# Batch 0 of a linear-attention and expert kernel: the query maxima subtracted by TensorE in PSUM, not by VectorE in SBUF

## The chip, the core and the metric

One Trainium2 chip, one core. The metric is the time of one execution in microseconds (us) on the device. The engines named below: PE (TensorE, matrix products; PEld is its weight load), DVE (VectorE), ACT (ScalarE), POOL (GpSimd) and SP (which issues most DMAs). Each engine works through its own queue in order; engines wait for each other by semaphores. PSUM has eight banks of 128 x 512 floats here.

## The reference, cut to what matters

Four batches of linear ("performer") attention over 8 heads, 576 tokens and 64 dimensions; then a dense layer of 2304 tokens (512 to 2048 to 512); then a layer of eight experts that is routed by argmax. The change touches the features of q:

```
def phi(x):                                   # x: q or k, scaled
    proj = np.einsum('bhsd,md->bhsm', x, omega)
    sq = np.sum(x * x, axis=-1, keepdims=True) / 2.0
    h = proj - sq
    h = h - np.max(h, axis=-1, keepdims=True)  # maximum over the 128 features
    return np.exp(h) / np.sqrt(m)
q_p, k_p = (phi(q_s), phi(k_s))
kv = np.einsum('bhsm,bhsd->bhmd', k_p, v)
num = np.einsum('bhsm,bhmd->bhsd', q_p, kv)   # divided by den = q_p . sum(k_p)
```

The term `sq` is the same for all features of a token, so it falls out when the maximum is taken away, and the kernel doesn't compute it.

## The kernel before

**Attention.** A batch is worked in four pairs of heads (p = 0 to 3). A pair of q lies as 128 rows, 64 for each of its two heads r, by 576 tokens. For k, the projection puts tokens on the partitions (L372), DVE takes the maxima (L378), ACT the exponentials (L393), and `k_kv` (L409) makes the 128 x 65 state kv, which ACT copies out of PSUM (`kv_copy`, L415). For q the projection puts the 128 features on the partitions:

- `q_proj` (L430): per head two products of 288 columns each, in four PSUM banks; the two heads use the two halves of the array's rows.
- `q_copy` (L458): ACT copies them to an SBUF tile `pr` of 128 x 576 for each head, and the banks are free.
- `q_max` (L466): POOL's partition_all_reduce puts the maximum over the features of each token into all 128 rows of a tile `mx`.
- `q_sub` (L471): DVE computes pr - mx. `q_exp` (L475): ACT takes the exponential of all 576 columns.
- `x_num` (L485, PE) multiplies by kv, `x_div` (L496 to L499, DVE) divides, `x_turn` (L508, PE) transposes, `x_hi` (L516, ACT) and `x_lo` (L520, DVE) write the result as a high and a low part, xh and xl.

The tiles `pr` have three buffers and a pair takes two, so the projections of pair p + 1 start when `x_num` of pair p has read its tiles.

**The dense layer.** A step (c, f) is `mm1` (L615) of a chunk of tokens and 128 of the 2048 hidden units, then the gate on ACT and DVE, then `mm2` (L646). Chunk 0 has 512 tokens, all from batch 0, so the first step, `mm1` of (0, 0), needs all four pairs of batch 0. While chunk 0 runs, its weights are still being converted from raw words to floats: 32 units, each a load on SP, two activations (L545, L551) and a cast (L588) on ACT, and four operations on DVE (L561, L563, L570, L592). Attention of batch 1 is interleaved with the steps of chunk 0; batches 2 and 3 come later.

**The order of the work.** Every operation is handed to a planner, `Schedule`, with an engine, a cost, a rank and the tiles that it needs; `plan` is a list scheduler that runs a model of the engines and writes out each engine's queue in that order. All tags of PSUM draw on the same eight banks. Before the first step, `warm_up` (L241) fills each gap that the planner sees on PE with small products of a zero tile, one for every 0.31 us of gap; they stand in PE's queue like any other work. `QPE`, empty here, would choose for a pair of heads another way to take the maxima.

Of the kernel before, what the change touches and what calls it, by code (L numbers as in the profile page):

```python
# [9 lines left out]
F32 = mybir.dt.float32  # L10
# [32 lines left out]
BIG = 1 << 20  # L43

QPE = ()
GS = 4
KPS = 4
VX = 2
# [149 lines left out]
def performer_moe_kernel(  # L198
# [52 lines left out]
    V.memset(idle, 0.0)  # L251
    ident = const.tile([128, 128], F32, name="ident")

    tri = const.tile([128, 128], BF16, name="tri")
    ones = const.tile([128, 128], BF16, name="ones")
    V.memset(ones, 1.0)
# [35 lines left out]
    st = {}  # L292
# [69 lines left out]
    def half(h):  # L362
        return slice(h * 64, h * 64 + 64)
# [54 lines left out]

    def q_cols(b, p, i):

        return slice(i * 384, 384 + i * 192) if (b, p) in QPE else slice(i * HS, (i + 1) * HS)

    def q_proj(b, p, i):
        c = q_cols(b, p, i)
        n = c.stop - c.start
        ps = [bank(b, "x") for _ in range(2)]
        qr = st["qr", b, p]
        if (b, p) not in QPE:
            for r in range(2):
                T.matmul(ps[r][:, 0:n], wb[half(r), :], qr[half(r), c], start=True, stop=True)  # L430
        else:

            for t in XG[i]:
                rows = rows_of(t)
                o = slice(t * 128 - c.start, t * 128 - c.start + rows)
                for r in range(2):
                    T.matmul(ps[r][:, o], wb[half(r), :], qr[half(r), t * 128:t * 128 + rows], start=True, stop=False)
                for r in range(2):
                    col = st["qm", b, p, t // 3, r][:, t % 3:t % 3 + 1]
                    T.matmul(ps[r][:, o], col.to_broadcast([128, M]), ident[:, 128 - rows:128], start=False, stop=True)  # L440
        for r in range(2):
            st["qps", b, p, r, i] = ps[r]
# [8 lines left out]
    def q_tile(b, p, r):  # L451
        if ("e", b, p, r) not in st:
            st["e", b, p, r] = at.tile([128, S], F32, tag="pr", bufs=3, name="pr")
        return st["e", b, p, r]

    def q_copy(b, p, r, i):
        c = q_cols(b, p, i)
        A.copy(q_tile(b, p, r)[:, c], st.pop(("qps", b, p, r, i))[:, 0:c.stop - c.start])  # L458

    def q_expp(b, p, r, i):  # L460
        c = q_cols(b, p, i)
# [719 lines left out]
    def dve(n):  # L1181
        return 0.06 + n * 1.05e-3
# [19 lines left out]
    def attention(b, start, period):  # L1202
        for p in range(4):
# [17 lines left out]
            add("SP", SPC, -5 if b else -9, load_v, (), seq="sv", w=["v"], tl=[("vx", 0)], nbytes=128 * 645 * 4)  # L1221
            d = AT["d0"] if b == 0 else AT["d"]
            mine = (b, p) in QPE
            parts = [(0, 0), (0, 1), (1, 0), (1, 1)]
            for g in range(2):
                banks = [(kind("att"), "k", g, h) for h in range(2)]
# [28 lines left out]
            for r in range(2):  # L1255
                v = u + 3.0 * r
                for i in range(2):
                    c = q_cols(b, p, i)
                    n = c.stop - c.start
                    bank_ = (kind("x"), "q", r, i)  # L1260
                    if mine:
                        add("ACT", act(n), u + i, q_expp, (r, i), r=[("qps", i)], w=[("e", i)], tl=[bank_, ("pr", r)])
                    else:
                        add("ACT", act(n), u + i, q_copy, (r, i), r=[("qps", i)] + [("qpr", r)] * i, w=[("qpr", r)],
                            tl=[bank_, ("pr", r)])
                if not mine:
                    add("POOL", 2.1, v, q_max, (r,), r=[("qpr", r)], w=[("qm", r)], tl=[("pr", r), ("mx", r)])
                    add("DVE", dve(S), v + 3, q_sub, (r,), r=[("qm", r)], w=[("qd", r)], tl=[("pr", r), ("mx", r)])
                    add("ACT", act(S), v + 3, q_exp, (r,), r=[("qd", r)], w=[("e", 0), ("e", 1)], tl=[("pr", r)])
            for g in range(2):  # L1270
# [267 lines left out]
```

## Time and profile before

| | us |
|---|---|
| median of three runs | 624.19 (622.95 to 625.39) |
| the profiled execution: its time, its span | 624.3, 622.4 |
| PE busy (share of the span) | 599.8 (96%) |
| DVE busy | 440.7 (71%) |
| ACT busy | 291.1 (47%) |
| POOL busy | 110.3 (18%) |
| mean granted TensorE clock | 0.991 |

Busy time on PE is to be read with care here: up to the first step it contains the fillers of L241, which compute nothing. A product of 32-bit floats is one row of the order and two records in the trace: the order has 63 fillers, the trace 126.

### The profile page before, as it was taken

How to read it: one execution, taken by the hardware profiler on the slowest of the kernel's cores; microseconds unless marked ns; L12 is line 12 of the kernel's file. 1: busy time of each engine (PE TensorE's matmuls, PEld its weight loads, DVE VectorE, ACT ScalarE, POOL GpSimd, SP SyncE). 2: the span in 40 equal slices, each digit the busy share in tenths (PEclk: the TensorE clock that was granted, in tenths of full speed). 3: DMA queues.
4: the chain of work that ended last, by engine and by line, in shares of the span. 5: the costliest groups of instructions: out<-in, count | busy, mean ns of one | idle time of the engine just before them, and what ended most of it. 6: DMA issues, size and time to landing. Idle time of an engine off the chain costs nothing. (4 is left out here: it accounts for less than half of the span.)

```text
span 622.4 us, 11811 instructions
## 1 busy us (share of the span) xinstructions
PE 599.8 (96%) x4350; PEld 510.6 (82%) x4350; DVE 440.7 (71%) x1198; ACT 291.1 (47%) x672; POOL 110.3 (18%) x83
## 2 busy tenths in 40 slices
PE   9899999999999999999999999799999999999994
PEld 8677777788888898889988888799899889797883
DVE  3889999998769969863269673549722887449861
ACT  4776988677532456442234653332222323443220
POOL 2225034000020022221002043100010002402431
PEclk9999999999999999999999999899999999999998
DMA  7566466366366346322334313124212423892311
GB/s 281 163 196 189 151 202 212 117 217 203 99 231 185 99 141 176 90 67 56 68 91 148 108 65 52 34 85 136 68 52 68 135 89 99 265 351 69 92 45 53
DMA packets 38412, 81.66 MB, mean 131 GB/s; under 512 B 5740, under 2 KB 6380, under 8 KB 38352
## 3 DMA queue, kind: packets, MB, share of 16 engines
q1 hardware_dynamic: 36144, 76.90, 40.1%
q0 software_dynamic: 1776, 3.56, 1.9%
q8 instruction: 35, 0.57, 0.4%
q10 hardware_dynamic: 432, 0.43, 0.2%
q14 instruction: 25, 0.20, 0.1%
HBM read 65.88 MB, written 15.25 MB: 130 GB/s over the span
## 5 line engine op out<-in xcount | busy, mean ns | idle before, releaser
L646 PE MATMUL acc<-wo,gh 128*128 128x512 f32 x576 | 184.2, 401 | 0.2 <-ACT gh L630 0.2
L661 DVE CUSTOM_DVE_ANT_0 idle<-x,wg 128x512 uint8<-128x512 f32 x162 | 115.2, 711 | 7.6 <-ACT x L652 4.5
L646 PEld LDWEIGHTS acc<-wo,gh 128*128 128x128 f32 x576 | 103.9, 188 | 20.0 <-ACT gh L630 0.8
L621 ACT ACTIVATE g<-mm,half_t 128x384 f32<-128x384 f32 (+2 forms) x96 | 55.8, 581 | 126.6 <-PE mm L615 118.9
L646 PE MATMUL acc<-wo,gl 128*128 128x512 f32 x288 | 114.4, 397 | 0.1
L466 POOL PARTITION_ALL_REDUCE mx<-pr x32 | 67.6, 2160 | 234.1 <-ACT pr L458 227.7
L626 DVE SCALAR_TENSOR_TENSOR g<-g,mm 128x384 f32<-128x384 f32 (+2 forms) x96 | 52.8, 551 | 66.1 <-ACT g L621 65.6
L615 PE MATMUL mm<-xh,wih 128*128 128x384 f32 (+2 forms) x384 | 85.3, 344 | 0.1
L630 ACT CAST gh<-g 128x384 fp32r<-128x384 f32 (+2 forms) x96 | 49.3, 514 | 73.4 <-PE acc L646 46.6
L615 PE MATMUL mm<-xl,wih 128*128 128x384 f32 (+2 forms) x384 | 82.5, 336 | 0.0
L636 DVE TENSOR_TENSOR gl<-g,gh 128x384 fp32r<-128x384 f32 (+2 forms) x96 | 53.3, 556 | 33.4 <-ACT gh L630 33.2
L615 PEld LDWEIGHTS mm<-xh,wih 128*128 128x128 f32 x384 | 67.8, 189 | 9.0 <-DVE xl L520 0.2
L615 PEld LDWEIGHTS mm<-xl,wih 128*128 128x128 f32 x384 | 66.7, 188 | 2.8
L615 PE MATMUL mm<-xh,wil 128*128 128x384 f32 (+1 forms) x320 | 66.0, 328 | 1.0 <-DMA wil<-wils 1.0
L646 PEld LDWEIGHTS acc<-wo,gl 128*128 128x128 f32 x288 | 54.1, 188 | 13.8 <-DVE gl L636 0.9
L739 POOL DMA_INDIRECT tab<-rec,r_sloti x18 | 18.4, 1024 | 211.4 <-DVE rec L735 177.3
L615 PEld LDWEIGHTS mm<-xh,wil 128*128 128x128 f32 x320 | 54.6, 188 | 1.3 <-DMA wil<-wils 1.3
L393 ACT ACTIVATE kp<-att,kmx 128x128 f32<-128x128 f32 x160 | 45.5, 384 | 14.9 <-DVE kmx L378 14.8
L471 DVE TENSOR_TENSOR pr<-pr,mx 128x576 f32<-128x576 f32 x32 | 31.3, 978 | 8.4 <-POOL mx L466 8.4
L378 DVE TENSOR_REDUCE kmx<-att 128x2 f32<-128x256 f32 (+1 forms) x64 | 28.1, 482 | 8.2 <-PE att L372 5.1
L475 ACT ACTIVATE pr<-pr 128x576 f32<-128x576 f32 x32 | 22.1, 690 | 22.3 <-DVE pr L471 21.6
L485 PE MATMUL att<-kv,pr 128*64 128x65 f32 x640 | 25.1, 234 | 4.8 <-ACT pr L475 4.2
(204 smaller groups left out, 768.2 us busy)
## 6 DMA issues: line engine op xcount, KB each, us to landing
wil<-wils SPq DMA_DIRECT2D x80, 256.0 KB
w<-w_in SPq DMA_DIRECT2D x16, 512.0 KB
w<-w_out SPq DMA_DIRECT2D x16, 512.0 KB
vx<-vn SPq DMA_DIRECT2D x16, 322.5 KB
qr<-qt SPq DMA_DIRECT2D x16, 288.0 KB
out<-x SPq DMA_DIRECT2D x18, 256.0 KB
x1d<-x SPq DMA_DIRECT2D x18, 256.0 KB
kr<-kt SPq DMA_DIRECT2D x15, 288.0 KB
```

The costliest lines, as they stand in the source:

```text
L378: V.reduce_max(out=mx[:, 0:n], in_=st[key, b, p, g, h][:, 0:n * M].rearrange("p (g m) -> p g m", m=M), axis=AX.X, negate=True)
L393: A.activation(kp[:, i], ps[:, i * M:(i + 1) * M], AF.Exp, bias=mx[:, i:i + 1], scale=1.0)
L466: G.partition_all_reduce(mx, st["e", b, p, r], channels=128, reduce_op=bass_isa.ReduceOp.max)
L471: V.tensor_sub(pr, pr, st.pop(("qm", b, p, r)))
L485: T.matmul(ps[m:m + 64, i * 130 + r * 65:i * 130 + r * 65 + 65], st["e", b, p, r][:, s0 + m:s0 + m + 64], kv[:, r * 65:(r + 1) * 65], star ...
L615: T.matmul(ps[:, 0:CHS[c]], w[:, k, :], x[:, k, d], start=(n == 0), stop=(n == 3 * KC - 1))
L621: A.activation(t, mmp[c, f][:, 0:CHS[c]], AF.Relu, bias=half_t, scale=2.0 ** -UP / 6.0)
L626: V.scalar_tensor_tensor(out=t, in0=t, scalar=1.0, in1=mmp.pop((c, f))[:, 0:CHS[c]], op0=ALU.min, op1=ALU.mult)
L630: A.copy(gh, gt[c, f])
L636: V.tensor_sub(gl, t, gh.bitcast(F32))
L646: T.matmul(accs[c, t], g[:, ts], w[:, r, f % 2, :], start=(f == 0 and j == 0), stop=(f == FT - 1 and j == 2))
L661: V.tensor_tensor_reduce(out=idle.bitcast(mybir.dt.uint8), in0=x1[i], in1=wg[:, e, :], scale=1.0, scalar=0.0, op0=ALU.mult, op1=ALU.add, a ...
```

## The change

A list `QSB` names the four pairs of batch 0. For them the projections are split 384 + 192 columns rather than 288 + 288, their PSUM banks aren't closed and aren't freed by the copy, POOL's maxima are taken as before, and then `q_subp` multiplies a constant `minus` (zero but for a row of -1 at row 0 and row 64) with `mx`, accumulating into the banks that still hold the projections: each bank then holds projection minus maximum. `q_expp`, which was there for `QPE`, takes the exponential from PSUM into `pr`. `q_sub` and `q_exp` go for these pairs; batches 1 to 3 keep them. `q_subp` needs the maxima of both heads. The numbers of the planner stay as they are, and it writes the queues anew with the new operations. POOL's queue comes out the same from end to end.

```diff
+QSB = ((0, 0), (0, 1), (0, 2), (0, 3))
...
+    minus = const.tile([128, 128], F32, name="minus")
+    V.memset(minus, 0.0)
+    for r in range(2):
+        V.memset(minus[r * 64:r * 64 + 1, :], -1.0)
...
-        return slice(i * 384, 384 + i * 192) if (b, p) in QPE else slice(i * HS, (i + 1) * HS)
+        return slice(i * 384, 384 + i * 192) if (b, p) in QPE + QSB else slice(i * HS, (i + 1) * HS)
...
-                T.matmul(ps[r][:, 0:n], wb[half(r), :], qr[half(r), c], start=True, stop=True)
+                T.matmul(ps[r][:, 0:n], wb[half(r), :], qr[half(r), c], start=True, stop=(b, p) not in QSB, skip_group_check=True)
...
-        A.copy(q_tile(b, p, r)[:, c], st.pop(("qps", b, p, r, i))[:, 0:c.stop - c.start])
+        key = ("qps", b, p, r, i)
+        A.copy(q_tile(b, p, r)[:, c], (st[key] if (b, p) in QSB else st.pop(key))[:, 0:c.stop - c.start])
+
+    def q_subp(b, p, i):
+
+        c = q_cols(b, p, i)
+        for r in range(2):
+            T.matmul(st["qps", b, p, r, i][:, 0:c.stop - c.start], minus[half(r), :], st["qm", b, p, r][half(r), c],
+                     start=False, stop=True, skip_group_check=True)
...
+                if sub and r == 1:
+                    for i in range(2):
+                        n = (384, 192)[i]
+                        add("PE", 0.05 + n * 2.2e-3, v + 3 + i, q_subp, (i,), mode="r", r=[("qm", 0), ("qm", 1)], w=[("qms", i)],
+                            tl=[(kind("x"), "q", k, i) for k in range(2)] + [("mx", k) for k in range(2)])
+                        for k in range(2):
+                            add("ACT", act(n), v + 3 + i, q_expp, (k, i), r=[("qms", i)], w=[("e", i)],
+                                tl=[(kind("x"), "q", k, i), ("pr", k)])
+                if not mine and not sub:
                     add("DVE", dve(S), v + 3, q_sub, (r,), r=[("qm", r)], w=[("qd", r)], tl=[("pr", r), ("mx", r)])
                     add("ACT", act(S), v + 3, q_exp, (r,), r=[("qd", r)], w=[("e", 0), ("e", 1)], tl=[("pr", r)])
```

**How the queues move.** Line numbers after the change are larger: `q_proj` is L437, the k projection L379, `k_kv` L416, the filler L243, `q_subp` L472, `q_copy` L466, `q_expp` L477, `x_num` L500, the k exponentials L400, the weights' activations L560 and L566, their cast L603, `mm2` L661, `mm1` L630, `x_turn` L523.

PE in pair 1 of batch 0, before, from the k projection of the next pair to the q projection of pair 2:

```order
L372 MATMUL att<-wb,kr 128x128 x10
L241 MATMUL acc<-idle 128x128 x9
L409 MATMUL acc<-vx,kp 64x65 x12
L241 MATMUL acc<-idle 128x128
L409 MATMUL acc<-vx,kp 64x65 x8
L241 MATMUL acc<-idle 128x128 x2
L485 MATMUL att<-kv,pr 64x65 x20
L430 MATMUL mm<-qr,wb 128x288 x4
```

and the same stretch after:

```order
L379 MATMUL att<-wb,kr 128x128 x6
L243 MATMUL acc<-idle 128x128 x5
L379 MATMUL att<-wb,kr 128x128 x4
L243 MATMUL acc<-idle 128x128
L416 MATMUL acc<-vx,kp 64x65 x12
L243 MATMUL acc<-idle 128x128 x2
L416 MATMUL acc<-vx,kp 64x65 x8
L472 MATMUL mm<-mx,minus 128x384 x2
L472 MATMUL mm<-mx,minus 128x192 x2
L243 MATMUL acc<-idle 128x128 x2
L500 MATMUL att<-kv,pr 64x65 x20
L437 MATMUL mm<-qr,wb 128x384 x2
```

Four subtracting products have come in, two fillers have gone, and the k projection is cut in two, with one PSUM bank for the fillers, one for kv and four held by q, two of the eight are left for it at a time.

ACT in the same pair, before, from the copies of q to the last exponential of q (`wo`, `wih` and `ca` belong to the conversion of the weights):

```order
L458 COPY pr<-mm 128x288 x4
L588 CAST wo<-ca 128x512
L393 ACTIVATE kp<-att,kmx 128x128 x8
L475 ACTIVATE pr<-pr 128x576
L393 ACTIVATE kp<-att,kmx 128x128 x2
L588 CAST wih<-ca 128x512
L475 ACTIVATE pr<-pr 128x576
```

and after:

```order
L466 COPY pr<-mm 128x384 x2
L466 COPY pr<-mm 128x192 x2
L603 CAST wo<-ca 128x512
L400 ACTIVATE kp<-att,kmx 128x128 x6
L603 CAST wih<-ca 128x512
L400 ACTIVATE kp<-att,kmx 128x128 x4
L560 ACTIVATE ca<-w_328 128x512
L422 COPY kv<-acc 128x130
L566 ACTIVATE w_328<-w_328 128x512
L477 ACTIVATE pr<-mm 128x384 x2
L477 ACTIVATE pr<-mm 128x192 x2
```

The exponentials of q now stand behind all ten of k, the copy of kv and two activations of the next unit of weights, and they are four pieces where there were two.

PE in batch 2, pair 1, before, between the projection of q and `x_num` (ahead of these rows stand four of L430, three of L508 and two of L646):

```order
L646 MATMUL acc<-wo,gl 128x512
L646 MATMUL acc<-wo,gh 128x512 x2
L646 MATMUL acc<-wo,gl 128x512
L508 MATMUL att<-ident,xn 128x128 x2
L646 MATMUL acc<-wo,gh 128x512 x2
L646 MATMUL acc<-wo,gl 128x512
L615 MATMUL mm<-xh,wih 128x384 x4
L615 MATMUL mm<-xl,wih 128x384 x4
L615 MATMUL mm<-xh,wil 128x384 x4
L409 MATMUL att<-vx,kp 64x65 x20
L372 MATMUL att<-wb,kr 128x128 x10
L485 MATMUL att<-kv,pr 64x65 x12
```

and after (ahead of these rows stand the second half of the projection, four of L379 and two of L661):

```order
L661 MATMUL acc<-wo,gl 128x512
L523 MATMUL att<-ident,xn 128x128 x5
L661 MATMUL acc<-wo,gh 128x512 x2
L661 MATMUL acc<-wo,gl 128x512
L630 MATMUL mm<-xh,wih 128x384 x4
L630 MATMUL mm<-xl,wih 128x384 x4
L630 MATMUL mm<-xh,wil 128x384 x4
L661 MATMUL acc<-wo,gh 128x512 x2
L661 MATMUL acc<-wo,gl 128x512
L379 MATMUL att<-wb,kr 128x128 x6
L416 MATMUL att<-vx,kp 64x65 x8
L500 MATMUL att<-kv,pr 64x65 x20
```

The projection of q stands nearer to the product that needs it: twelve of L409 and four of L372 less between them. Past the middle of batch 2 the order of PE, DVE, ACT and SP is that of before.

## Rows read from the trace of the kernel before

**Rows 1.** Busy time of each engine in three stretches, with granted clock and DMA.

```profile
0.00:58.60 58.60, 52.85 (x649) 44.36 (x649) 42.99 (x110) 40.69 (x113) 19.28 (x14) 0.97 0.63 207
58.60:122.00 63.40, 60.95 (x548) 46.12 (x547) 60.16 (x124) 49.74 (x113) 16.31 (x8) 1.00 0.55 176
...
262.00:622.40 360.40, 346.46 (x2175) 302.40 (x2169) 218.45 (x659) 124.09 (x274) 58.16 (x52) 0.99 0.33 99
```

**Rows 2.** PE in order of time, batch 0: start, length, line, operation.

```profile
22.15 1.24 PE L430 MATMUL mm<-qr,wb 64*128 64x288 f32 x8
...
32.29 2.12 PE L485 MATMUL att<-kv,pr 128*64 128x65 f32 x40
34.34 1.24 PE L430 MATMUL mm<-qr,wb 64*128 64x288 f32 x8
...
44.62 1.24 PE L430 MATMUL mm<-qr,wb 64*128 64x288 f32 x8
...
53.48 1.67 PE L485 MATMUL att<-kv,pr 128*64 128x65 f32 x40
...
58.60 1.18 PE L615 MATMUL mm<-xh,wih 128*128 128x512 f32 x4
```

**Rows 3.** What PE waited for up to 60 us, longest first.

```profile
PE acc L409 <- ACT kp L393: 1.8, 3, 0.9
```

**Rows 4.** POOL in order of time, the maxima of batch 0.

```profile
10.99 3.92 POOL L466 PARTITION_ALL_REDUCE mx<-pr  x2 [9.53 <-ACT pr L458]
24.20 4.66 POOL L466 PARTITION_ALL_REDUCE mx<-pr  x2 [9.29 <-ACT pr L458]
36.22 4.37 POOL L466 PARTITION_ALL_REDUCE mx<-pr  x2 [7.36 <-ACT pr L458]
46.50 4.12 POOL L466 PARTITION_ALL_REDUCE mx<-pr  x2 [5.90 <-ACT pr L458]
```

**Rows 5.** Groups by line up to 58.6 us: busy us, mean ns, idle before.

```profile
L241 PE MATMUL acc<-idle 128*128 128x128 f32 x126 | 21.2, 321 | 1.1 <-DVE idle L251 1.1
...
L393 ACT ACTIVATE kp<-att,kmx 128x128 f32<-128x128 f32 x50 | 14.6, 391 | 6.7 <-DVE kmx L378 6.6
L471 DVE TENSOR_TENSOR pr<-pr,mx 128x576 f32<-128x576 f32 x8 | 7.3, 917 | 0.0
...
L551 ACT ACTIVATE w<-w 128x512 int32<-128x512 uint32 x8 | 5.7, 711 | 0.0
L545 ACT ACTIVATE ca<-w 128x512 f32<-128x512 f32 x8 | 5.6, 705 | 0.0
L475 ACT ACTIVATE pr<-pr 128x576 f32<-128x576 f32 x8 | 5.6, 702 | 0.8 <-DVE pr L471 0.8
L430 PE MATMUL mm<-qr,wb 64*128 64x288 f32 x32 | 5.4, 429 | 0.0
L458 ACT COPY pr<-mm 128x288 f32<-128x288 f32 x16 | 5.4, 418 | 2.2 <-PE mm L430 2.2
...
L516 ACT CAST xh<-mm 128x384 fp32r<-128x384 f32 x4 | 2.0, 501 | 1.4 <-PE mm L508 1.4
L516 ACT CAST xh<-mm 128x192 fp32r<-128x192 f32 x4 | 1.3, 335 | 0.3 <-PE mm L508 0.2
```

**Rows 6.** DVE in order of time, two operations while POOL takes maxima.

```profile
24.80 1.38 DVE L561 TENSOR_SCALAR ca<-ca 128x512 int32<-128x512 int32 x1
...
38.80 1.59 DVE L471 TENSOR_TENSOR pr<-pr,mx 128x576 f32<-128x576 f32 x1
```

**Rows 7.** PE in order of time, its two longest waits from 58.6 to 122 us.

```profile
78.44 0.93 PE L372 MATMUL att<-wb,kr 64*128 64x128 f32 x10 [0.58 <-DVE xl L520]
...
118.90 0.55 PE L508 MATMUL att<-ident,xn 128*128 128x128 f32 x3 [0.96 <-DVE xn L499]
```

**Rows 8.** PE in order of time, batch 2: a q projection and its x_num.

```profile
236.75 1.24 PE L430 MATMUL att<-qr,wb 64*128 64x288 f32 x8
...
246.21 0.92 PE L485 MATMUL att<-kv,pr 128*64 128x65 f32 x24
```

More of the change, by code (lines that the diff above doesn't have):

```diff
@@ L1223, in attention @@
             mine = (b, p) in QPE
+            sub = (b, p) in QSB
             parts = [(0, 0), (0, 1), (1, 0), (1, 1)]
```

## The prediction

> **What bounds the kernel now.** I read the busy time by stretch first. From 58.6 us on PE hardly stops: in 58.6 to 122 it is idle for 63.40 - 60.95 = 2.45 us [rows 1]. What stands in PE's queue from there on is real work, and the change leaves its amount alone. So the time is the start of the first step, 58.60 us [rows 2], plus a train of PE work that is fixed but for its idle gaps.
>
> Ahead of 58.60 PE looks busy too (52.85 of 58.60, rows 1), but 21.2 us of that are the 63 fillers [rows 5], and 58.60 - 52.85 = 5.75 us are idle. So this stretch isn't bound by PE's work, nor by DVE (42.99 busy), ACT (40.69) or POOL (19.28) [rows 1]. It is bound by a chain that runs four times: q projection, copies, two maxima on POOL, subtraction, exponential, `x_num`, and then the projection of the next pair, since the `pr` tiles come free only there. The projections start at 22.15, 34.34 and 44.62: 12.2 and 10.3 us for a turn [rows 2], of which POOL holds 4.1 to 4.7 [rows 4].
>
> The place of the change is the link from the end of POOL to `x_num`. Pair 1: POOL ends at 24.20 + 4.66 = 28.86, `x_num` starts at 32.29, so 3.43 us. Pair 3: 46.50 + 4.12 = 50.62 to 53.48, so 2.86 us [rows 2, 4]. The bare work there is a subtraction of about 0.75 us (median; 7.3 us for eight with the stretched ones) and an exponential of 0.70 [rows 5], 1.45 together. The rest is queueing.
>
> **The change, part by part.** The profiled execution took 624.3 us with its span of 622.4, and lies 0.1 above the median of 624.19. The sum is made against 624.3.
>
> *DVE loses eight subtractions*, 7.3 us [rows 5]. It isn't full in this stretch (42.99 of 58.60), so this isn't 7.3 us of time. It is used up by conversions that move forward: up to the last `x_lo` of batch 0 the new order has eight units begun where there were seven. The three small fills of `minus` lie at the very start, before DVE has any data to work on. Nothing.
>
> *PE gains eight subtracting pairs of products*, with the same columns and the same half arrays as the projections of q: 5.4 us for the four pairs by that group [rows 5]. It loses eight fillers (63 to 55): 8 x 21.2 / 63 = 2.7 us [rows 5]. So its queue ahead of the first step grows by 2.7 us. The 5.75 us of idle time hide this; if that cover is gone, the first step comes up to 2.7 us later. In the queue, `q_subp` waits for both heads' maxima, and behind it stand half of a k projection or of `k_kv`, which ACT and DVE wait for in turn. In the order it comes after enough fillers and k work that POOL is done or nearly so; I count no wait of its own.
>
> *ACT*: eight exponentials of 576 columns (5.6 us) become sixteen of 384 and 192. The nearest rows are the casts from PSUM of the same widths, 0.50 and 0.34: 8 x 0.84 = 6.7 us, so 1.1 more. The copies cost the same: 0.50 + 0.34 against 2 x 0.42 [rows 5]. All this is beside other work but for what lies on the link.
>
> *The link itself.* Its bare work is now two thirds of a 1.24 us projection [rows 2], 0.83 us, and then the two 384-column exponentials in series, 1.00 us [rows 5], since `x_num` needs both heads: 1.83 us against 1.45. Against the measured links the most that can be won is 3.43 - 1.83 = 1.60 in pair 1 and 2.86 - 1.83 = 1.03 in pair 3. But ACT's queue must let them through. In pair 1 it now has, between the copies and the exponentials of q, ten exponentials of k at 0.29 us, two casts and two activations of 512 columns at about 0.71 [rows 5], and the small copy of kv: 2.9 + 2.8 + 0.3 = 6.0 us, where POOL needs 4.66 [rows 4]. So the exponentials start at least 1.3 us after POOL's end and `x_num` some 2.3 us after it, before any wait; the k exponentials also wait for DVE's maxima (6.6 us in all up to 58.6, rows 5), and PE's `k_kv` waits for them (1.8 us, rows 3). I take 4.0 us there: 0.6 lost. In pair 3 the queue is shorter (two casts, two activations, six exponentials: 0.84 + 1.42 + 1.74 = 4.0 us, under POOL's 4.12), so I take 0.6 won of the possible 1.03. Pairs 0 and 2 I leave at nothing. Ahead of the first step there is one filler more, 0.3 us. So the first step moves by +0.3 us. Bounds: -3.6 (the bare link in pairs 1 and 3, half of the smaller gain in each of the other two) and +2.7 (PE's queue, cover gone).
>
> *After the first step.* DVE is one unit of conversion ahead, and of the 2.45 us that PE idles up to 122 us, its two longest waits are both for DVE, 0.58 and 0.96 us [rows 7]. I take back 0.5. Bounds: -2.4 (all of it) and +1.5 (two such waits more, since the order in this stretch is new).
>
> *Batch 2.* In pair 1 PE had 246.21 - (236.75 + 1.24) = 8.2 us from the end of the projection to `x_num` [rows 8]. The new order takes twelve products of `k_kv` and four of the k projection out from between them, which leaves about 6.9 us. What must fit in is a copy of 0.42, POOL's 3.9 to 4.7, 0.75 and 0.70 [rows 4, 5]: 5.8 to 6.5 us without any queueing. That is tight: +0.5, bounds 0 and +2.0. Later on the order is that of before, so nothing.
>
> Sum: 624.3 + 0.3 - 0.5 + 0.5 = 624.6.
>
> *A rule beside the rows.* POOL's two maxima take 3.92 us in pair 0, but 4.66, 4.37 and 4.12 in the others [rows 4], and a subtraction that falls into POOL's time took 1.59 us [rows 6]. But a weight conversion did so too: 1.38 us at 24.80, just when POOL began [rows 6]. The Trainium skill, "SBUF — State Buffer", Who interferes with whom, says that VectorE with two SBUF inputs contends with a GpSimd operation that reads SBUF, and that the second of them is blocked for the whole of the first; by that rule the subtractions, which read two SBUF tiles, could be what slows POOL. With all maxima at 3.92, the chain would be 0.74 + 0.45 + 0.20 = 1.4 us shorter, and the time 623.2. I don't put it into the sum: the conversions that move into these places are stretched by POOL just as well, and no row shows POOL's slowing to be the subtractions' doing. It would still be "no change".
>
> **Rivals.**
>
> *Faster: the queueing on DVE was the pace of batch 0.* DVE waits for nothing through much of each turn, and the subtractions queue behind conversions there; without them the link falls to its bare work. First step -3.6: 624.3 - 3.6 - 0.5 + 0.5 = 620.7, or less if PE's idle time up to 122 us goes too. For it: 2.86 to 3.43 us where the work is 1.45. Against it: the exponentials leave one queue to stand in another, and the turn is held by the k exponentials as well.
>
> *Slower: PE's queue is the pace.* The four held banks cut the k projections in two, `q_subp` stands in front of `k_kv`, and the fillers are executed whether or not there is a gap. Then the 2.7 us of added queue come out whole, and the tight place of batch 2 costs 1.0: 624.3 + 2.7 + 1.0 = 628.0. It decides from the point at which PE's idle time ahead of the first step can't shrink by the 2.7 us that come in, that is, where over 3 us of the 5.75 stay. For it: 1.8 us of it are waits of `k_kv` for ACT [rows 3], and ACT gets 1.1 us more to do. Against it: before, PE had the time.
>
> *The change does nothing*, because POOL's 4.1 to 4.7 us and ACT hold the turn: that is my forecast. The rule above, at 623.2, lies within it.
>
> **How the numbers follow.** A measurement of this kernel can tell about 0.5% from no change, 3.1 us: below 621.1 is faster, above 627.3 slower. Forecast 624.6: 0.44. The rule on POOL, 623.2: 0.09. Faster, 620.7: 0.25. Slower, 628.0: 0.22. That makes 0.25 faster, 0.53 the same, 0.22 slower. The range reaches to the middle of both rivals and takes in their likelier half: 620.5 to 628.2. All bounds together would be 624.3 - 3.6 - 2.4 = 618.3 and 624.3 + 2.7 + 1.5 + 2.0 = 630.5; I leave those ends to the 2 in 10.
>
> **What would show it.** The start of the first `mm1` in the new trace: 58.9 if I am right, 55 to 56 for the faster rival, 61 for the slower one. The link from POOL's end to `x_num`: about 4 us in pair 1, 2.3 in pair 3; under 2 in all of them for the faster rival. Idle time of PE ahead of the first step: 3 to 4 us by my sum (5.75 + 0.3 - 2.7), 5 or more for the slower rival. Idle time from there to 63 us later: about 2. The waits of `x_num` in batch 2: under 1 us. What would make the prediction wrong without any of this is a wait past 262 us: PE is idle for 14 us there [rows 1], and if transfers fall otherwise, a gap of that kind may grow or go though its order is unchanged.

## The result, and the profile after

The changed kernel took 627.62 us (median of nine runs, 625.9 to 627.99), the kernel before 622.95 on the same chip (nine runs, 622.25 to 625.39): a ratio of 1.0063, 95% interval 1.0047 to 1.0079. So it is slower by 0.6%. The time lies in the range, but near its end: outside the 0.5% of my likeliest case, and close to the 628.0 of the slower rival.

Its profiled execution took 627.62 us with a span of 625.8: 3.4 us over the span before. Busy time by stretch, the columns as in rows 1 (PE, PEld, DVE, ACT, POOL, then granted clock, DMA share, GB/s), up to the first step and for 63.4 us from there:

```profile
0.00:60.22 60.22, 54.35 (x665) 44.92 (x665) 39.17 (x110) 41.84 (x122) 18.08 (x14) 0.97 0.65 210
60.22:123.62 63.40, 59.87 (x545) 44.81 (x544) 59.57 (x122) 49.33 (x114) 16.20 (x8) 1.00 0.55 179
```

Against rows 1: ahead of the first step PE is busy 1.50 us more and idle 60.22 - 54.35 = 5.87 us, where it was 5.75; behind it PE is idle 3.53 us, where it was 2.45. DVE has 3.8 us less to do ahead of the first step, and that isn't where the time was.

POOL's maxima of batch 0, which answer to rows 4, and one DMA that SP issues:

```profile
10.08 3.92 POOL L481 PARTITION_ALL_REDUCE mx<-pr  x2 [8.61 <-ACT pr L466]
22.77 4.28 POOL L481 PARTITION_ALL_REDUCE mx<-pr  x2 [8.77 <-ACT pr L466]
36.54 3.91 POOL L481 PARTITION_ALL_REDUCE mx<-pr  x2 [9.49 <-ACT pr L466]
47.00 1.96 POOL L481 PARTITION_ALL_REDUCE mx<-pr  x1 [6.55 <-ACT pr L466]
51.15 1.96 POOL L481 PARTITION_ALL_REDUCE mx<-pr  x1 [2.19 <-DMA tab<-empty]
...
44.84 0.38 SPq L332 DMA_DIRECT2D tab<-empty  x1
```

In pair 3 the second maximum waits 2.19 us for a DMA. The tile `empty`, from which the table in DRAM is cleared, has the tag of POOL's `mx` tiles, two buffers for both, and the new order clears the table ahead of this maximum; before, it came behind it. PE in order of time, the first step and the longest waits around it (the idle time and who ended it stand in brackets), which answer to rows 2, 3 and 7:

```profile
26.52 0.71 PE L379 MATMUL att<-wb,kr 64*128 64x128 f32 x6 [1.60 <-ACT kp L400]
...
30.64 1.81 PE L472 MATMUL mm<-mx,minus 64*128 64x384 f32 x8
...
33.03 1.39 PE L500 MATMUL att<-kv,pr 128*64 128x65 f32 x40
...
53.17 0.91 PE L472 MATMUL mm<-mx,minus 64*128 64x384 f32 x4 [1.80 <-POOL mx L481]
...
60.22 1.18 PE L630 MATMUL mm<-xh,wih 128*128 128x512 f32 x4
...
80.54 1.57 PE L379 MATMUL att<-wb,kr 64*128 64x128 f32 x20
...
86.45 1.20 PE L630 MATMUL mm<-xh,wih 128*128 128x512 f32 x4 [1.34 <-ACT kp L400]
```

The first step starts 1.62 us later. In pair 1, `q_subp` (L472) starts at 30.64, where POOL was done at 22.77 + 4.28 = 27.05. And the fourth step (86.45) waits 1.34 us for ACT's exponentials of k: the k projection at 80.54 now stands in one piece of four banks, and `mm1` gets its bank only when exponentials free one. Before, that projection came in three pieces and the step waited for nothing:

```profile
83.47 1.21 PE L615 MATMUL mm<-xh,wih 128*128 128x512 f32 x4
```

Two of PE's waits in the changed kernel from 60 us on (in total, times, the longest):

```profile
PE att L500 <- ACT pr L490: 3.9, 3, 3.0
PE mm L630 <- ACT kp L400: 1.6, 2, 1.3
```

The second is new. The first is `x_num`; 3.6 us of it are a gap of batch 3 that the kernel before has too (4.0).

A step's second group of products (xl by wih) can be followed through all traces. The table gives how much later (+) it starts than in the kernel before, at five steps. Each row of the table is a single profiled execution, and the beginning of the program alone differs by more than 1 us between executions (see below the table).

| kernel | 59.62 | 84.52 | 107.42 | 266.11 | 519.33 |
|---|---|---|---|---|---|
| changed | +1.61 | +2.97 | +2.30 | +2.66 | +3.39 |
| e1, own buffer for the table | +0.56 | +1.65 | +0.99 | +1.36 | +1.83 |
| e4, e1 with the tail of before | +0.96 | -0.26 | -0.24 | -0.29 | -0.16 |
| e6, tail of the changed kernel alone | -0.19 | +3.41 | +2.71 | +3.04 | +3.05 |
| e2, subtractions cut | -2.58 | -2.59 | -2.58 | -2.60 | -2.18 |
| e3, products alone | +1.90 | +1.88 | +1.89 | +1.85 | +2.22 |
| e5, fillers at that place | -0.79 | -0.80 | -0.79 | -0.82 | -0.56 |
| e7, half the fillers | -1.84 | -2.29 | -2.27 | -2.30 | -1.25 |
| e8, maxima before puts | -1.02 | -1.05 | -1.04 | -1.06 | -6.78 |
| e9, changed, and as e8 | +1.52 | +2.87 | +2.20 | +2.56 | -3.23 |
| e11, e4 and as e8 | +1.23 | +0.03 | +0.04 | -0.05 | -5.80 |
| e10, e7 and e8 | -4.31 | -3.88 | -3.88 | -3.95 | -9.72 |

For the changed kernel it reads: 1.6 us ahead of the first step, 0.7 up to 107 us, 0.4 from there to 266 us, and 0.7 at a gap of batch 3 around 395 us where the order is unchanged.

Two things that are not the edits' doing move every column. The first is the opening of the program: thirteen fillers that stand ahead of the first k projection in the queue of both kernels.

```profile
1.05 5.81 PE L241 MATMUL acc<-idle 128*128 128x128 f32 x26 [1.05 <-DVE idle L251]
```

```profile
1.05 4.81 PE L243 MATMUL acc<-idle 128*128 128x128 f32 x26 [1.05 <-DVE idle L253]
```

They took 5.81 us in the trace before and 4.81 in that of the changed kernel, 5.62 in e1, which has the changed kernel's queues, and 4.53 to 5.92 in the other traces that have all thirteen. Why isn't shown. The second is the clock. The kernel before, the changed one, e4, e6, e9 and e11 show the lower level (a granted clock of 0.5) for some 3 us between 27 and 34 us; e1, e2, e5 and e8 show none there. So like is compared with like if the time is counted from the start of POOL's first maximum, and traces with that low stretch are set against each other (us):

| from POOL's first maximum | to the first step | to the step at 266.11 |
|---|---|---|
| *with the low stretch* | | |
| kernel before | 47.61 | 255.12 |
| e6, beginning of before, new order behind it | 47.56 | 258.29 |
| e4, changed beginning, old order behind it | 49.78 | 256.03 |
| e11, the same | 49.82 | 256.04 |
| changed | 50.14 | 258.69 |
| e9, changed up to here | 50.15 | 258.69 |
| *without it* | | |
| e8, kernel before up to here | 46.39 | 253.86 |
| e1, changed, own buffer for the table | 48.29 | 256.60 |

So the changed beginning costs 2.2 us up to the first step (1.9 without the low stretch), and the wait for the table 0.35 more: 2.53 in all, of which 0.91 came back in the opening, so that 1.62 is left in the table of five steps. At 266 us the changed beginning with the old order behind it is 0.9 us late, and the new order adds 2.3.

### The profile page after: what moved, and what is told of

The parts are those of the page before. It is cut to its first block, busy times and chain, and to the rows that moved or that the text cites. A ratio compares the mean times of both kernels' runs of the same rounds, so it can differ in the third digit from the quotient of the medians.

```text
span 625.8 us, 11874 instructions
## 1 busy us (share of the span) xinstructions
PE 602.3 (96%) x4366; PEld 510.6 (82%) x4366; DVE 434.1 (69%) x1193; ACT 290.5 (46%) x680; POOL 109.7 (18%) x83
## 5 line engine op out<-in xcount | busy, mean ns | idle before, releaser
L661 PE MATMUL acc<-wo,gh 128*128 128x512 f32 x576 | 184.2, 400 | 0.2
L661 PEld LDWEIGHTS acc<-wo,gh 128*128 128x128 f32 x576 | 104.0, 188 | 19.9 <-ACT gh L645 1.0
L661 PE MATMUL acc<-wo,gl 128*128 128x512 f32 x288 | 114.4, 397 | 0.1
L630 PE MATMUL mm<-xh,wih 128*128 128x384 f32 (+2 forms) x384 | 85.9, 345 | 1.6 <-ACT kp L400 1.6
L630 PE MATMUL mm<-xl,wih 128*128 128x384 f32 (+2 forms) x384 | 83.1, 338 | 0.0
L651 DVE TENSOR_TENSOR gl<-g,gh 128x384 fp32r<-128x384 f32 (+2 forms) x96 | 55.2, 575 | 35.8 <-ACT gh L645 35.5
L630 PEld LDWEIGHTS mm<-xh,wih 128*128 128x128 f32 x384 | 67.8, 189 | 11.7 <-ACT kp L400 2.4
L630 PEld LDWEIGHTS mm<-xl,wih 128*128 128x128 f32 x384 | 67.2, 190 | 2.7
L630 PE MATMUL mm<-xh,wil 128*128 128x384 f32 (+1 forms) x320 | 66.3, 329 | 0.7 <-DMA wil<-wils 0.7
L661 PEld LDWEIGHTS acc<-wo,gl 128*128 128x128 f32 x288 | 54.1, 188 | 14.1 <-DVE gl L651 1.2
L630 PEld LDWEIGHTS mm<-xh,wil 128*128 128x128 f32 x320 | 55.0, 189 | 1.0 <-DMA wil<-wils 1.0
L400 ACT ACTIVATE kp<-att,kmx 128x128 f32<-128x128 f32 x160 | 45.8, 386 | 16.3 <-DVE kmx L385 15.5
L385 DVE TENSOR_REDUCE kmx<-att 128x3 f32<-128x384 f32 (+1 forms) x64 | 28.2, 482 | 13.1 <-PE att L379 7.9
L379 PE MATMUL att<-wb,kr 64*128 64x128 f32 x320 | 27.9, 287 | 2.8 <-ACT kp L400 1.6
L379 PEld LDWEIGHTS att<-wb,kr 64*128 64x128 f32 x320 | 23.3, 187 | 7.9 <-issue 2.8
L486 DVE TENSOR_TENSOR pr<-pr,mx 128x576 f32<-128x576 f32 x24 | 23.4, 977 | 8.3 <-POOL mx L481 8.2
```

What stands on the lines that cost most here:

```text
L379: T.matmul(st[key, b, p, g, h][:, i * M:(i + 1) * M], x[half(h), min(c * 128, S - 128):min(c * 128 + 128, S)], wb[half(h), :], start=True, ...
L385: V.reduce_max(out=mx[:, 0:n], in_=st[key, b, p, g, h][:, 0:n * M].rearrange("p (g m) -> p g m", m=M), axis=AX.X, negate=True)
L400: A.activation(kp[:, i], ps[:, i * M:(i + 1) * M], AF.Exp, bias=mx[:, i:i + 1], scale=1.0)
L486: V.tensor_sub(pr, pr, st.pop(("qm", b, p, r)))
L630: T.matmul(ps[:, 0:CHS[c]], w[:, k, :], x[:, k, d], start=(n == 0), stop=(n == 3 * KC - 1))
L651: V.tensor_sub(gl, t, gh.bitcast(F32))
```

## The experiments

Theory when I began: the loss is the wait for the table. Rivals: PE's longer queue ahead of the first step, and the new order behind it.

**e1: the table in a buffer of its own.** All queues stay as in the changed kernel.

```
-        empty = at.tile([128, TABN // 128 + 1, 2], I32, tag="mx", bufs=2, name="empty")
+        empty = gp.tile([128, TABN // 128 + 1, 2], I32, tag="g", bufs=GS, name="empty")
```

> The changed kernel with one edit: the table of 153 pairs of words that is filled in batch 0 (`empty`) lies in a buffer of the tag `g` and not in one of the two `mx` buffers of POOL's maxima; the queues of all engines are the same, row for row. Theory A (the eighth maximum of batch 0 waited 2.19 us for the transfer of that table, and the first step waited for that maximum): the second maximum of pair 3 begins right behind the first, near 49.0 us, the first step at 58.2 to 58.6 us in place of 60.22, and the whole is 1.6 to 2.0 us shorter than the changed kernel, about 625.8, 1.003 of before. Theory B (the 2.7 us that the subtracting products add to PE's queue set the first step): it stays at 60.2 us and the time at 627.6.

Measured: 626.3 us, ratio to the kernel before 1.0058 (1.0039 to 1.0078). POOL's row of pair 3, and the first step:

```profile
46.23 4.06 POOL L481 PARTITION_ALL_REDUCE mx<-pr  x2 [6.53 <-ACT pr L466]
...
59.16 1.18 PE L630 MATMUL mm<-xh,wih 128*128 128x512 f32 x4
```

The wait is gone, the loss is not: 1.0058 for 1.0063. The theory falls as the main cause; the table is worth 0.35 us by the traces above, which the two ratios, each to 0.2%, can't tell from nothing.

**e4: the changed beginning with the old order behind it.** e1, and from the first `mm1` on every engine's queue in the order of the kernel before (the planner runs for both, and the rest is sorted by the other's list).

```
+            done = order[:cut + 1]
+            rest = [(i, 0.0) for i, _ in order[cut + 1:]]
+            order = done + sorted(rest, key=lambda o: at[names[o[0]]])
```

> e1_own_buffer, and from the first step on every engine works in the order of the kernel before (the planner is run for both kernels, and what stands behind the first mm1 is sorted by the order of the other). Theory A (of the 3.4 us between the two profiles 1.6 came ahead of the first step, 0.7 from the new order up to 122 us and 0.3 from the new order of batch 2): first step at 58.2 to 58.6, PE idle 2 to 2.5 us from there to 63 us later, and the time within 0.5 us of before, 622.5 to 623.5. If the loss behind the first step is not from the order, but from what the conversions and the banks are like when the first step starts: 0.7 to 1.0 us more, the time of e1.

Measured: 624.81 us, 1.0024 (1.0002 to 1.0045), 0.34% less than e1. Its first and fourth step:

```profile
59.57 1.17 PE L651 MATMUL mm<-xh,wih 128*128 128x512 f32 x4
...
83.23 1.20 PE L651 MATMUL mm<-xh,wih 128*128 128x512 f32 x4
```

I had expected its first step at 58.2 to 58.6 and 622.5 to 623.5 us in all; both came later. Up to the fourth step 1.2 us of the loss were made good, if the order behind is the old one: 0.67 us of them show as idle time of PE, 0.82 us from the first step to the one at 107.42, where it was 1.49, since its waits for DVE fell from 1.0 to 0.4. So that DVE's lead is the reason of the whole is likely and not shown. Counted from POOL's first maximum 0.9 us are left, beside the 0.24% (1.5 us) of the runs. In the new order (e1) nothing is made good: the fourth step, at 85.14, has the same wait of 1.34 us as the changed kernel, and PE is idle for 2.70 us in that stretch.

**e6: the new order alone.** The other half: the beginning of the kernel before, and from the first `mm1` on the order of the changed kernel; the table is in the buffer that it has in both. Against e4:

```
-    QSB, sc = keep, fresh()
+    QSB, sc = (), fresh()
```

> The complement of the run with the tail of the kernel before: up to the first mm1 all engines stand in the order of the kernel before, subtractions on DVE included, and from there on in the order of the changed kernel (the k projection of batch 1, pair 2 in one piece of four banks). Theory A, the new order behind the first step costs by itself: ratio to the kernel before 1.002 to 1.0045 (the two runs with the changed beginning differ by 1.0058 to 1.0024), first step unmoved, and mm1 waits over 1 us for a bank of the k projection (released by ACT's exponentials of k) between 60 and 122 us. Rival, that difference came with the beginning or from chance: ratio 0.999 to 1.001.

Measured: 626.35 us, 1.006 (1.0041 to 1.0079). PE's two longest waits after the first step:

```profile
68.06 1.22 PE L682 MATMUL acc<-wo,gh 128*128 128x512 f32 x2 [2.32 <-ACT gh L666]
...
86.89 1.20 PE L651 MATMUL mm<-xh,wih 128*128 128x512 f32 x4 [0.93 <-ACT kp L421]
```

The new order costs by itself, even more than expected, but the run isn't clean. This beginning lacks DVE's lead of one unit of conversion, which then stands at the head of the new tail; the 2.32 us at 68.06, and a granted clock of 0.60 at 68 to 72 us, probably come of that. The wait for the bank is there too, at 0.93 us. So the size of the order's cost is taken from e1 against e4, and from e9 against e11 below.

**e2: DVE's share.** The kernel before with the subtractions of batch 0 cut to 32 of 576 columns.

```
-        V.tensor_sub(pr, pr, st.pop(("qm", b, p, r)))
+        n = 32 if b == 0 else S
+        V.tensor_sub(pr[:, 0:n], pr[:, 0:n], mx[:, 0:n])
```

> The kernel before, with the eight subtractions of batch 0 cut from 576 to 32 columns (the other columns of the maxima are left unsubtracted, so part of the computation is left out); queues the same. It shows what taking the subtractions off DVE is worth by itself. Theory A (they were hidden but for what lies on the link): the first step comes 0 to 1.5 us earlier than 58.60, the time is 621.5 to 623. The rival that DVE's queue paced batch 0: 3 us earlier or more, 619.5.

Measured: 621.91 us, 0.9992 (0.998 to 1.0003). Counted from POOL's first maximum the first step comes after 45.56 us, 0.83 less than in e8, which has the old subtractions and no low clock either; the runs give 0.5 us. So little was to be won on DVE, as I had forecast. Its maxima on POOL:

```profile
23.68 4.65 POOL L466 PARTITION_ALL_REDUCE mx<-pr  x2 [9.30 <-ACT pr L458]
34.36 4.45 POOL L466 PARTITION_ALL_REDUCE mx<-pr  x2 [6.03 <-DVE ca L562]
```

They take as long as with the whole subtractions (4.66 and 4.37, rows 4; 4.65 and 4.45 in e8). And in pair 0 of the kernel before, a whole subtraction falls into POOL's time, which is 3.92 us all the same:

```profile
13.43 1.28 DVE L471 TENSOR_TENSOR pr<-pr,mx 128x576 f32<-128x576 f32 x1
```

What goes with POOL's longer times is another operation of DVE, a conversion that reads two tiles (L563), here in pair 2 of the kernel before:

```profile
36.13 0.69 DVE L563 SCALAR_TENSOR_TENSOR ca<-w,ca 128x512 int32<-128x512 int32 x1
```

In all thirteen traces a pair of maxima of batch 0 takes 3.91 or 3.92 us where no such conversion overlaps it, and 3.97 to 4.66 where one does. The changed order has none beside pair 2 (3.91) and still has one beside pair 1 (4.28). No run moved this conversion alone.

**e3: PE's share.** The kernel before, with the products of `minus` and `mx` added at the place of the second subtraction, into the bank of the fillers. The subtractions stay on DVE.

```
+        if b == 0 and r == 1:
+            for c in (slice(0, 384), slice(384, 576)):
+                T.matmul(warm[0][:, 0:c.stop - c.start], minus, mx[:, c], start=True, stop=True)
```

> The kernel before, with four pairs of products minus times mx (384 and 192 columns, whole array, one head for each pair of heads) added into the fillers' bank, where the subtraction of the second head stands; nothing reads them. About 1.0 us of PE work for each pair of heads, 4 us in all, and PE waits for the maximum of the second head. It shows what the added work on PE is worth by itself. Theory A (PE's idle time hides it): the first step moves by less than 1 us, the time by less than 1 us (ratio 0.999 to 1.002). Theory B (PE's queue is the pace): first step 2.5 to 4 us later, 625.5 to 627.

Measured: 625.86 us, 1.0052 (1.0035 to 1.0068): theory B by the time; the first step comes 1.90 us later, which is less than B had. PE at the place of pair 3, and the windows there:

```profile
49.94 1.59 PE L479 MATMUL acc<-mx,minus 128*128 128x384 f32 x4 [1.83 <-POOL mx L471]
51.32 3.73 PE L241 MATMUL acc<-idle 128*128 128x128 f32 x20
```

```profile
48.00:50.00 2.00, 0.17 (x3) 0.06 (x1) 2.00 (x4) 0.35 (x1) 1.89 (x1) 1.00 0.86 241
50.00:52.00 2.00, 2.00 (x8) 1.74 (x9) 1.90 (x6) 1.98 (x7) 0.00 (x0) 0.67 0.84 218
52.00:54.00 2.00, 2.00 (x11) 2.00 (x11) 1.53 (x4) 2.00 (x9) 0.00 (x0) 0.50 0.53 205
```

PE stands 1.83 us before the products until POOL is done, and then the granted clock falls to 0.67 and 0.50, the lower of its two levels (1.2 GHz): the ten fillers behind take 3.73 us, where they took 2.50 in the kernel before.

**e5: the same work, without the wait.**

```
+        if b == 0 and r == 1:
+            for _ in range(4):
+                T.matmul(warm[0][:, 0:128], idle, idle, start=True, stop=True)
```

> The kernel before, with four fillers more per pair of batch 0 (0.33 us each), put in PE's queue at the place where the run before this one had its two products of minus and the maxima. They read a constant tile and wait for nothing, so 1.3 us a pair of PE work is added without the wait for POOL; the output is the reference's. Theory A, PE's queue is the pace of batch 0: most of the price stays, the first step starts 1.5 to 3 us later than in the kernel before (granted clock taken into account), ratio 1.0025 to 1.005. Rival, the price of the products was PE's wait for POOL's maxima (2.8 us in two waits) and what queued behind it: without the wait the idle time takes the work in, first step under 0.7 us later, ratio at most 1.0015.

Measured: 623.0 us, 1.0001 (0.9985 to 1.0018): the rival. Busy time up to the first step, of this kernel and of e8, which has the same beginning without the 16 fillers:

```profile
0.00:57.82 57.82, 53.90 (x681) 46.08 (x681) 43.07 (x110) 40.83 (x113) 19.35 (x14) 1.00 0.64 210
```

```profile
0.00:57.58 57.58, 51.75 (x648) 43.24 (x649) 42.96 (x110) 40.72 (x113) 19.34 (x14) 1.00 0.64 211
```

PE is busy 2.15 us more and idle 1.91 us less, and counted from POOL's first maximum the first step comes 0.41 us later (46.80 for 46.39). Work that waits for nothing goes nearly all into the idle time. So PE's longer queue by itself isn't the cause; and since e3's products take about as long as these fillers (1.24 and 1.16 us in pair 1), e3's loss is put down to the wait in PE's queue and the clock after it.

**e7: half the fillers**, in the kernel before.

```
-            for _ in range(int((gap - 0.1) / AT["fill"])):
+            for _ in range((int((gap - 0.1) / AT["fill"]) + 1) // 2):
```

> The kernel before with half as many fillers in each gap (36 for 63 ahead of the first step, some 9 us less work in PE's queue); nothing else is touched. Theory A, PE's queue is the pace, and fillers are executed whether or not there is a gap: those right ahead of an x_num, a projection or the first step, 6 fewer at 0.32 us, come out of the time: first step 1.5 to 3 us earlier, ratio 0.995 to 0.998. Rival 1, the chain over POOL, ACT and DVE is the pace: first step within 0.7 us, ratio 0.999 to 1.001. Rival 2, the clock: without the fillers TensorE is granted its lower level in more stretches ahead of the first step than the one at 30.5 to 34 us, and the first step comes 1 to 4 us later, ratio 1.002 to 1.006.

Measured: 621.21 us, 0.9967 (0.9948 to 0.9987). The size is A's, the reason only in part. POOL's first maximum starts at 9.26 us, where it was 10.99 (rows 4), and from there to the first step it takes 47.50 us, where it was 47.61. So the gain that shows stands at the opening, where seven fillers are left of thirteen; openings with all thirteen put that maximum at 9.79 to 11.19. In the links the clock was low in three stretches instead of one, and what fewer fillers gave there it took: e10 below, with the same fillers and one low stretch, takes 45.68 us, 0.7 less than e8 without any.

**e8: the gap in batch 3.** In the kernel before, PE is idle for 3.22 and 0.80 us at 388 to 392.7 for the exponentials of pair 3 of batch 3, since POOL holds three `route_put` transfers ahead of its maxima. The edit puts the three behind them.

```profile
391.57 0.34 PE L485 MATMUL att<-kv,pr 128*64 128x65 f32 x4 [3.22 <-ACT pr L475]
392.70 2.22 PE L485 MATMUL att<-kv,pr 128*64 128x65 f32 x36 [0.80 <-ACT pr L475]
```

```
+        moved = [o for o in order if o[0] in puts]
+        order = [o for o in order if o[0] not in puts]
+        at = next(n for n, o in enumerate(order) if o[0] == last) + 1
+        order = order[:at] + moved + order[at:]
```

> The kernel before with one exchange on POOL in batch 3: the three route_put transfers that stand ahead of the two maxima of pair 3 (at 376.6, 380.8 and 386.1 us in the kernel before) come behind them. Theory: the 4.0 us that PE idles at 388 to 392.7 for that pair's exponentials and the lower clock after it are one stall made by POOL's queue; it goes whole: time 3 to 5.5 us less, ratio 0.991 to 0.995, and no granted clock under 0.9 at 384 to 404 us. That would also say that the 0.75 us more that the changed kernel's trace lost there is this stall's clock and none of the change. Rival, the time is given back at a later wait (a transfer or PE's bank): gain under 1.5 us, ratio above 0.9975.

Measured: 617.19 us, 0.9901 (0.9867 to 0.9934). POOL there, before and then in e8:

```profile
386.07 0.97 POOL L739 DMA_INDIRECT tab<-rec,r_sloti  x1 [4.28 <-DMA tab<-rec,r_sloti]
387.06 3.88 POOL L466 PARTITION_ALL_REDUCE mx<-pr  x2
```

```profile
378.37 3.91 POOL L479 PARTITION_ALL_REDUCE mx<-pr  x2 [8.43 <-ACT pr L471]
382.45 0.99 POOL L752 DMA_INDIRECT tab<-rec,r_sloti  x1 [0.17 <-issue]
```

The gap goes whole, and its clock with it: 5.7 us in the table for 4.02 us of waiting, a little more than expected. No other single edit here won as much, and the change doesn't touch this place.

**e9: the changed kernel with the exchange of e8.**

> The changed kernel with the same exchange on POOL in batch 3 as in the run that put the maxima before the route_put transfers. Theory: the 0.73 us that the changed kernel's trace lost around 395 us was the lower clock after that stall and no part of the change: the kernel gains 6 to 7 us as the kernel before did (616.5 to 617.9 there), 620 to 621.5 us, ratio to the kernel before 0.9955 to 0.9985, and 2.5 to 4 us behind that kernel with the same exchange. Rival, the changed kernel loses more at that place for a reason of its own: gain 5 us or less, 622.5 us or more.

Measured: 621.05 us, 0.9957 (0.9937 to 0.9977). Against the 1.0063 of the changed kernel without it that is 1.06% less, about as much as e8 gained (0.99%). So the 0.73 us at 395 us went with the gap: they were its clock, which stayed at 0.50 from 394 to 400 us in that trace and at 0.57 to 0.58 from 392 to 396 in the trace before. But the changed kernel stays 0.56% behind e8 (each ratio to 0.2 or 0.3%); the cause lies elsewhere.

**e11: e4 with the exchange of e8.**

> The changed beginning (its own buffer for the table, the order of the kernel before from the first mm1 on) with the exchange on POOL in batch 3. Theory: the subtraction by PE alone costs what stood between 0.2 and 0.24% before: 617.5 to 619.5, 0.5 to 2.5 us behind the kernel before with the same exchange. Rival, the lead of DVE makes up for the later first step: within 0.4 us of that kernel, 616.8 to 617.6.

Measured: 618.09 us, on a chip on which the kernel before took 623.89: 0.9903 (0.987 to 0.9936), for 0.9901 (0.9867 to 0.9934) of e8. By the ratio it is the rival, but intervals of 0.3% can't tell it from the theory's 0.08 to 0.4%. For the theory speak e4 (1.0024, just clear of 1) and the traces: from POOL's first maximum to the step at 266.11, e4 and e11 both take 0.9 us more than the kernel before. So with the old order behind it the change gains nothing, and probably loses 0.9 us. In the new order (e9) it is 0.54% slower than that.

**e10: what is left to win.** The kernel before with the edits of e7 and e8.

> The kernel before with both edits that made it faster: the maxima of batch 3, pair 3 before the route_put transfers (ratio 0.9901) and half the fillers (0.9967). If the two stretches are independent, 0.987: 614 to 616 us. If fewer fillers only traded queue for a lower clock, 617 to 619.

Measured: 614.43 us, 0.9853 (0.982 to 0.9885), as for two independent stretches. It beats both kernels, and neither of its edits has to do with the maxima.

## Why the prediction was right or wrong, point by point

The range, 620.5 to 628.2, holds the measured 627.62, but not by the merit of the sum: 624.6 lies 3.0 us below it, and by my own line (above 627.3) this is the slower case, to which I gave 0.22. The upper end of the range came from a rival whose price the runs don't bear out. That it holds is in part luck.

**The first step: +0.3 predicted, +1.62 measured, +2.53 counted from POOL's first maximum.** Three of the four links from POOL's end to `x_num` came out longer. The steps that failed are these:

- "Pairs 0 and 2 I leave at nothing": pair 0 took 16.37 - 14.00 = 2.37 us, where it was 1.80, and pair 2 2.98, where it was 2.28. I had worked out that the bare link grows from 1.45 to 1.83 us, and then used that only as a bound of what can be won. In e1 it is 1.8 to 2.2 us from the start of `q_subp` to `x_num` in pairs 0 to 2, where the whole link of pair 0 was 1.80.
- Pair 1: 4.0 predicted, 5.98 measured, and 4.45 in e1 with the clock at 1.00. "I count no wait of its own" failed here: not for POOL, but PE's queue keeps `q_subp` from its work, behind the k projection that waits 1.60 us for ACT and the `k_kv` behind it (26.52 to 30.64 above). Before, the k projection stood in one piece there and waited for nothing; now four banks are held and it has to wait until ACT has read one of the two that are left, a cut that the slower rival had named and the sum had not priced. PE's lower clock after the wait took the rest, and I had put no clock into the sum; the trace before shows such a fall too, so it isn't the change's doing alone.
- Pair 3: "0.6 won of the possible 1.03". It is 0.45 won if counted from POOL's end, but that end came late: `q_subp` waits 1.8 us for it, the longest wait of PE up to 60 us. I hadn't seen that `empty` shares the buffers of `mx`, though the new order of SP and DVE shows the table ahead of the maximum. With a buffer of its own (e1) the link is 53.81 - 50.29 = 3.52 us: 0.66 lost.
- "The copies cost the same": all four together do (1.31 us in pairs 2 and 3, before and after), but POOL starts 2.54, 2.20 and 2.20 us after the projection starts in pairs 1 to 3, where it was 2.05, 1.88 and 1.88 (rows 2 and 4 against the rows above). That is 1.1 us in three pairs, and e1, e4 and e11 have it too. The first products and copies are now 384 columns wide, not 288, which is the likely reason; no run varied the split alone.

Two things spoke for the change and weren't in my sum. In pair 0 the next projection starts 3.86 us after `x_num`, where it took 5.44: DVE divides 1.15 us after `x_num`, not 2.73, since a conversion and seven small operations that stood ahead of the division come at another place now. And POOL's maxima took 0.38 and 0.46 us less in pairs 1 and 2 (4.28 and 3.91, for 4.66 and 4.37). The rule of the Trainium skill, "SBUF — State Buffer", Who interferes with whom, on which the 623.2 stood, would explain that by the missing subtractions; e2, where the subtractions are as good as gone, has 4.65 and 4.45, so they aren't the cause. The moved conversion goes with it (see e2).

**DVE: "Nothing".** Nearly right ahead of the first step: e2 gives 0.08%, and no change lies within its interval.

**PE's longer queue: "the 5.75 us of idle time hide this".** The idle time didn't shrink (5.87 us), which was my sign for the slower rival, and the time is the rival's. Yet the price that the rival put on it, 2.7 us of added queue that come out whole, is refuted by e5: 16 fillers at that place cost 0.01% (to 0.17%). What doesn't go into idle time is a product that itself waits, with work behind it (e3, 0.52%). Of the rival's other reasons the held banks did count (pair 1 above). So the time came near the rival's 628.0 by another sum than the rival's.

**After the first step: -0.5 predicted, +0.7 measured up to 107 us.** Here the sign was wrong. That some time would be made good was right, and more than I took, but only with the old order: 1.2 us (e4: +0.96 to -0.24; e11: +1.23 to +0.04). The new order takes that and 0.4 to 0.7 more (e1, e9, the changed kernel). I had read the new order for what moves ahead of waits, and not for banks: a k projection in one piece holds four of eight banks until ACT's exponentials have read them, and the `mm1` behind it waits 1.3 us. My bound of +1.5 allowed for such waits; the sum took none. By the runs the order is worth 0.34% (e1 against e4) to 0.54% (e9 against e11, with the wait for the table in it), each difference good to 0.3 or 0.4%; by the traces it is 2.3 us of the 3.6 lost at 266 us. So it is the larger part of the 0.63%. That the four banks are the reason within the order is read from the wait; no run cut that projection in pieces again.

**Batch 2: +0.5 predicted**, +0.36 measured from 107 to 266 us. The size is near by luck, since the wait that I had priced isn't what cost it: `x_num` of pair 1 waits 0.25 us (for ACT, at 249.93), and in its place went a wait of 0.26 for DVE that PE had before (at 245.57). PE is idle for 1.30 us in this stretch, where it was 1.42. Where the 0.36 arose isn't shown.

**Past it: nothing.** It was +0.73 at 395 us, of the kind that the last sentence of the prediction had named, and no part of the change (e9).

The chances, 0.22 for slower, were too low for one more reason: I had priced a new order by its amount of work, and in pair 1, at the table and at the fourth step it lost by what stands ahead of what.

What stays open: why the clock fell in pair 1 in six of the nine traces that have no fillers or products more or fewer than the two kernels, though e1 and e4 have the same queues and the same wait of 1.60 us there; why the opening took 1.00 us less in the changed kernel's trace; and whether the conversion that goes with POOL's longer maxima is their cause.

## What to carry to other kernels

When work moves to another engine, price the new chain from the last input to the next consumer in every turn, not only where the old one was long, and take only work that waits for nothing as hidden in idle time. Where a planner orders the queues anew, look through the new order for shared buffers: whose tag a moved tile has, and how many PSUM banks stand filled ahead of a product that needs one. And before tuning a link, look for the longest gap of the bound engine: here it was worth some ten times the 0.5 us that the subtractions on DVE cost, and it was made by the queue of an engine that is busy 18% of the time.

## What the runs showed of the hardware that I had not expected

- A wait of PE can cost more than its length. In these traces the granted clock fell after some waits to the lower level (1.2 GHz) for 3 to 7 us: the gap of 4.02 us cost 5.7 us (e8). The fall isn't sure: in 28 to 30 us, after the same wait, e1 was granted 1.00 and e4 0.50:

```profile
28.00:30.00 2.00, 2.00 (x35) 1.69 (x36) 1.52 (x4) 1.83 (x7) 0.00 (x0) 1.00 0.42 103
```

```profile
28.00:30.00 2.00, 2.00 (x22) 1.66 (x20) 1.06 (x3) 1.32 (x4) 0.00 (x0) 0.50 0.98 319
```

- Fillers that are to hold the clock up can be halved here at a gain of 0.33% (e7), though the clock is then low in more stretches.
- Two maxima of 128 x 576 on POOL take between 3.91 and 4.66 us, and the subtractions on DVE don't decide which (e2); in all traces the longer times go with one conversion on DVE (L563) that falls beside them.
- The same row of thirteen fillers at the start of the program took 4.53 to 5.92 us in different traces, at a granted clock that reads 1.00 throughout.
